# An attention and soft-MoE kernel: q and first-layer weights in longer packets, 32x32 score tiles, single ranks, late turning of combine weights

## The chip, the cores and the metric

One core of one Trainium2 chip. The metric is the device time in microseconds of one launch, the median of the runs shown. The engines are named as in the profile: PE (TensorE matmuls; PEld its weight loads), DVE (VectorE), ACT (ScalarE), POOL (GpSimd), SP (SyncE, which issues all DMA transfers here).

## The reference

```python
# q, k, v: [8 batches, 8 heads, 576, 64]; phi: [8, 8, 576, 32]; float32
a = softmax(phi, axis=2)                      # over the 576 tokens
k_m, v_m = a^T k, a^T v                       # 32 memory slots per head
attn = softmax(q k_m^T / 8, axis=-1)          # over the 32 slots
x = heads side by side of attn v_m            # [4608 tokens, 512]
logits = x @ moe_phi                          # [4608, 32]: 8 experts, 4 slots each
slot_input = softmax(logits, axis=0)^T x      # over all tokens
slot_out[e] = relu(slot_input[e] @ w1[e]) @ w2[e]    # w1: 512 x 1024, w2: 1024 x 512
out = softmax(logits, axis=1) @ slot_out      # [4608, 512]
```

## The kernel before

Every step is handed to a planner (`Plan.add`) with an engine, a cost, the tiles that it reads and writes and a rank. The planner walks through a modelled time and writes out one fixed order of instructions for each engine; ready steps of one engine go by rank. Ranks come from the table `AT` and from counters. The engines then run in that order and wait on semaphores. All DMA transfers stand on SP's queue, in the planner's order, and a load waits there until its buffer is free.

*Attention.* The 8 batches are worked in 4 pairs. A batch has phi, k, v and q loaded (`load_phi`, `load_kv`, `load_q`), 128 partitions by 4 chunks c of two heads each; 64 partitions hold one head, 9 tokens (j) each. phi's maximum is taken on DVE, spread by PE and ACT, subtracted on POOL and exponentiated on ACT (`shifted`); POOL adds up the sums (`summed`). `pooled` (L704) makes the 32 memory keys and values of each head on 64x32 PE tiles and ACT scales them into kp and vm. `turned` transposes kp (L748) and vm (L755), ACT copies them out (L762, L771), and PE multiplies the values by the routing matrix (L781). q is turned in blocks of 32x32 by DVE (`turn_q`, L591). For each pair and each chunk c, `scores` (L813) gives 128 partitions by 2 x 288 scores: 8 matmuls on 64x64 tiles, where the keys stand twice in a block-diagonal form (kps, whose other blocks are set to zero at the start), because the 64 partitions of one head hold two halves of its tokens. `softmax` takes it through DVE, POOL, ACT and back, `logits` (L882) sums the routing logits, and `route` weighs the tokens of a pair into the slot inputs (L1010, L1046, L1054, L1085). After the last pair, DVE merges the four pairs into SIM (L1233), the slot inputs of all experts.

*Experts.* 16 first-layer tiles of 1 MB (`expert_in`, L1353), 11 second-layer tiles of 1 MB (`expert_out`, L1413) and 5 more in quarters of 256 KB (`tail_out`, `tail_mult`), first the left 256 columns of the output (d = 0, in kvbank), then the right ones (d = 1, in scbank). The tiles share the arena, into which the weights are loaded as the attention's buffers come free. With each of the last six whole second-layer tiles a filler matmul (`keep_warm`, L1399) is handed in at a late rank.

*Output.* `slots` makes the combine weights of a pair, has PE turn them (L1523: five transposes a pair) and has ACT cast them into cT (L1535, L1538, L1539). `slot_sums` sums one half of the columns (L1325); then PE multiplies by the combine weights (L1594), ACT and DVE copy the results out (L1570, L1571) and SP stores them (L1607, L1687): six groups of three rows of tokens left, the same six right, then 18 rows whole.

Of the kernel before, what the change touches and what calls it, by code (L numbers as in the profile page):

```python
# [17 lines left out]
FILL = 10 ** 6  # L18
# [252 lines left out]
def kernel(  # L271
# [72 lines left out]
    KP_W = R * (P + Y)  # L344
# [65 lines left out]
    kbs, vTs = stack([2, C, R, M], 4, fifo=True), stack([C, R, M], 2)  # L410
# [33 lines left out]
    NWARM = 40  # L444
# [53 lines left out]
    DMA_RATE, IN_RATE, HALF_RATE, SPREAD = 412e3, 386e3, 350e3, 1.0  # L498

    def load(dst, src, nbytes, w, pri=None):  # L500
        add(
            SP, 0.06, lambda: nc.sync.dma_start(dst(), src), w=[w],  # L502
            dma=nbytes / {1 << 20: DMA_RATE, 1 << 18: HALF_RATE}.get(nbytes, IN_RATE), pri=pri, slack=SPREAD if nbytes == 1 << 18 else 0.0,
        )


    FIRST = ["phi0.0", "phi1.0", "mphi", "q0.0", "k0.0", "v0.0", "q1.0", "k1.0", "v1.0"]
# [30 lines left out]
    add(POOL, 3.6, f, r=[mphi_b], w=[mphd_b])  # L538
# [6 lines left out]
    class Batch:  # L545
# [32 lines left out]
        def load_q(self, u):  # L578
            qt, c0, c1 = self.qt, u * self.ks, u * self.ks + self.ks
            load(  # L580
                lambda: qt.ap.rearrange("p (c x) -> p c x", c=C)[:, c0:c1],
                rows(q, self.b)[:, c0:c1], H * S * D * 4 / self.units,
                qt if self.units == 1 else qt.part(u), pri=first(f"q{self.b}.{u}"),
            )
# [107 lines left out]
        def pooled(self, u):  # L692
# [6 lines left out]
            def f(js):  # L699
                for j in js:  # L700
                    for c in range(c0, c1):
                        for a in range(2):
                            h0 = HALF * a
                            nc.tensor.matmul(  # L704
                                acc.ap[M * c: M * c + M, a, : 2 * D],
                                ph()[h0: h0 + HALF, c, j, :],
                                kv()[h0: h0 + HALF, :, c, j * D: j * D + D],
# [5 lines left out]
            for js in (range(0, 3), range(3, 6), range(6, 9)):  # L713
                add(
                    PE, (0.075 * len(js) * self.ks, 8 * len(js) * self.ks), lambda f=f, js=js: f(js),
                    r=[pt.part(u), kvt.part(u), kvt.part(self.units + u)], w=[acc], also=[kp, vm],
                )

            def f():
                for a in range(2):  # L720
                    nc.scalar.activation(
                        kp.ap[o: o + n].rearrange("p i (r x) -> p i r x", r=R)[:, :, :, HALF * a: HALF * a + Y],
                        acc.ap[o: o + n, a, :D].rearrange("p (i x) -> p i x", i=2).unsqueeze(2)
                        .to_broadcast([n, 2, R, Y]),
                        AF.Copy, scale=rs.ap[o: o + n, a: a + 1],
                    )
                for a in range(2):
                    nc.scalar.activation(  # L728
                        vm.ap[o: o + n, a], acc.ap[o: o + n, a, D: 2 * D], AF.Copy,
                        scale=rs.ap[o: o + n, a: a + 1],  # L730
                    )

            add(
                ACT, 2 * act(P) + 2 * act(D), f, r=[acc, rs.part(u)],
                w=[kp.part(u), vm.part(u)],
            )

        def turned(self, u, vpb):
            kp, vm, kd, vT, n, o, g = self.kp, self.vm, self.kd, self.vT, self.n, u * self.n, self.g
            c0, c1, ks = u * self.ks, u * self.ks + self.ks, self.ks  # L740
            tp, tv, vpp = b_m.tile(), b_m.tile(), b_m.tile()
            ii = ident[o: o + n, o: o + n]

            def f():
                x = tp.ap.rearrange("p (i c r m) -> p i c r m", i=2, c=C, r=R)
                for i in range(2):
                    for r in range(R):
                        nc.tensor.transpose(  # L748
# [389 lines left out]
    for bp in range(NBP):  # L1138
# [19 lines left out]
        for h in range(2):  # L1158
            plan.at(bp + at["turn"][h])
            for x in pair:  # L1160
                x.turn_q(h)
# [530 lines left out]
```

## Time and profile before

| | |
|---|---|
| median of 3 runs | 202.4 us (202.2 to 202.49) |
| the profiled execution: time, span | 202.39 us, 200.6 us |
| PE, DVE, POOL, ACT busy | 172.5, 134.4, 84.3, 70.3 us |
| moved by DMA | 76.47 MB, mean 381 GB/s |
| mean granted clock of TensorE | 0.973 |

A row of a view gives start, duration, engine, line and operation, output tile and input tile; in brackets how long the engine stood idle before it and what ended that. A tile's name is that of its buffer: nearly all SBUF tiles lie in `arena`. A matmul in float32 runs in two passes, so it stands as two records of PE and two of PEld; transposes stand as one. DMA share is the mean busy share of the core's 16 DMA engines; where packets overlap it goes over 1.

### The profile page before, as it was taken

To read this page: it belongs to the slowest core of one execution; us is meant where nothing else is said; L and a number is where in the kernel's file an instruction comes from. 1 tells how busy PE (TensorE), PEld (TensorE's weight loads), DVE (VectorE), ACT (ScalarE), POOL (GpSimd) and SP (SyncE) were. 2 spreads that over 40 slices of the span, in tenths; PEclk is the share of its full clock that TensorE was granted. 3 is DMA by queue.
4 is the path that set the end of the run, shared out by engine and by line. 5 is a ranking of instruction groups with operands and counts; after the bars stand their busy time and mean duration, and the time that the engine had idled before them with its cause. 6 is when DMAs were issued, how large, how long until landed. Compare 5 with 4: busy or idle time off the path is not lost.

```text
span 200.6 us, 6083 instructions
## 1 busy us (share of the span) xinstructions
PE 172.5 (86%) x2623; PEld 111.0 (55%) x2623; DVE 134.4 (67%) x243; ACT 70.3 (35%) x188; POOL 84.3 (42%) x84
## 2 busy tenths in 40 slices
PE   7999748978699899797999789799999999999930
PEld 6777534636457387464665347464655654557520
DVE  6822640799897899999899996478990110558810
ACT  2022314546341755607463252110201123356600
POOL 7199204589992994889964276000000000000000
PEclk9999997899969999999999999999999999999995
DMA  5999999999999999999999999999999999999996
GB/s 201 362 394 395 381 384 389 381 390 379 397 379 390 389 382 396 383 391 398 404 412 401 409 408 411 408 430 418 415 418 421 378 321 329 356 331 312 398 426 279
DMA packets 34090, 76.47 MB, mean 381 GB/s; under 512 B 2064, under 2 KB 15888, under 8 KB 32400
## 3 DMA queue, kind: packets, MB, share of 16 engines
q1 hardware_dynamic: 34064, 76.09, 100.7%
q8 instruction: 20, 0.33, 0.7%
q14 instruction: 6, 0.05, 0.1%
HBM read 66.65 MB, written 9.44 MB: 379 GB/s over the span
## 4 chain that ended last, share of the span: by engine, by line
PE 34%; DMA 26%; DVE 13%; POOL 11%; issue 4%; SPq 4%; ACT 2%; POOLq 1%; DVEq 0%
DMA arena<-in_moe_w_dram 18%; DMA arena<-in_v_dram 8%; PE bank L1594 6%; PE scbank L813 6%; PE kvbank L704 5%; SPq L502 4%; PE bank L882 4%; POOL arena L848 3%; POOL arena L669 3%; POOL arena L648 3%; POOL arena L871 3%; PE bank L1010 2%; DVE arena L606 2%; DVE arena L827 2%; DVE arena L874 2%
## 5 line engine op out<-in xcount | busy, mean ns | idle before, releaser
L648 POOL TENSOR_TENSOR arena<-arena 128x1152 f32<-128x1152 f32 x8 | 21.0, 2633 | 17.6 <-ACT arena L641 15.1
L591 DVE STREAM_TRANSPOSE arena<-top 128x1152 f32<-128x1152 f32 x16 | 21.6, 1355 | 8.4 <-DMA top<-in_q_dram 8.4
L704 PE MATMUL kvbank<-arena 64*32 64x128 f32 x1152 | 21.2, 279 | 6.1 <-issue 2.9
L520 PE MATMUL kvbank<-ones 128*128 128x256 f32 x82 | 23.7, 426 | 2.4 <-ACT arena L728 1.3
L813 PE MATMUL scbank<-arena 64*64 64x288 f32 x256 | 23.8, 445 | 2.2 <-DVE arena L827 2.1
L669 POOL TENSOR_TENSOR arena<-arena 128x128 f32<-128x128 f32 (+2 forms) x32 | 23.4, 732 | 3.2 <-ACT arena L657 1.3
L704 PEld LDWEIGHTS kvbank<-arena 64*32 64x32 f32 x1152 | 16.5, 107 | 10.8 <-issue 5.9
L871 POOL TENSOR_TENSOR arena<-arena,ssm 128x576 f32<-128x576 f32 x16 | 18.3, 1155 | 9.5 <-DVE ssm L867 7.9
L848 POOL TENSOR_TENSOR arena<-arena,smx 128x576 f32<-128x576 f32 x16 | 18.4, 1153 | 7.6 <-DVE smx L843 7.6
L882 PE MATMUL bank<-arena 128*128 128x288 f32 x64 | 18.8, 425 | 1.3 <-DVE arena L874 0.8
L606 DVE TENSOR_REDUCE arena<-arena 128x128 f32<-128x1152 f32 x8 | 17.1, 2148 | 3.7 <-DMA arena<-in_phi_dram 3.6
L520 PEld LDWEIGHTS kvbank<-ones 128*128 128x128 f32 x82 | 15.9, 209 | 6.1 <-ACT arena L728 1.7
L1571 DVE COPY arena<-bank 128x256 f32<-128x256 f32 (+1 forms) x30 | 14.2, 510 | 5.9 <-PE bank L1594 5.8
L827 DVE STREAM_TRANSPOSE arena<-scbank 128x576 f32<-128x576 f32 x16 | 12.2, 765 | 5.4 <-PE scbank L813 5.4
L1594 PE MATMUL bank<-sr,cT 64*128 64x256 f32 (+1 forms) x104 | 14.7, 355 | 0.7 <-DVE arena L1571 0.6
L813 PEld LDWEIGHTS scbank<-arena 64*64 64x64 f32 x256 | 9.8, 139 | 10.1 <-DVE arena L827 3.6
L853 ACT ACTIVATE arena<-arena 128x576 f32<-128x576 f32 x16 | 11.0, 685 | 11.2 <-POOL arena L848 11.0
L882 PEld LDWEIGHTS bank<-arena 128*128 128x128 f32 x64 | 11.2, 189 | 6.4 <-issue 1.7
L1353 PE MATMUL bank<-arena,SIM 128*32 128x256 f32 x224 | 13.2, 390 | 0.4 <-DVE SIM L1233 0.4
L1594 PEld LDWEIGHTS bank<-sr,cT 64*128 64x128 f32 x104 | 9.9, 185 | 6.4 <-DVE arena L1571 4.6
L1570 ACT COPY arena<-bank 128x256 f32<-128x256 f32 (+1 forms) x24 | 10.3, 445 | 8.4 <-PE bank L1594 7.0
L874 DVE STREAM_TRANSPOSE arena<-arena 128x576 f32<-128x576 f32 x16 | 11.9, 754 | 1.5 <-POOL arena L871 1.5
(139 smaller groups left out, 249.2 us busy)
## 6 DMA issues: line engine op xcount, KB each, us to landing
arena<-in_moe_w_dram SPq DMA_DIRECT2D x25, 1024.0 KB, 14.5
top<-in_q_dram SPq DMA_DIRECT2D x8, 1152.0 KB, 12.6
arena<-in_k_dram SPq DMA_DIRECT2D x8, 1152.0 KB, 10.1
arena<-in_v_dram SPq DMA_DIRECT2D x8, 1152.0 KB, 12.5
arena<-in_moe_w_dram SPq DMA_DIRECT2D x20, 256.0 KB, 6.0
arena<-in_phi_dram SPq DMA_DIRECT2D x8, 576.0 KB, 7.2
out_dram<-arena SPq DMA_DIRECT2D x11, 384.0 KB, 3.4
out_dram<-arena SPq DMA_DIRECT2D x1, 2304.0 KB, 8.1
```

What stands on the lines that cost most here:

```text
L520: lambda: nc.tensor.matmul(warm.ap, ones, ones.unsqueeze(1).to_broadcast([P, 2, P]), start=True, stop=True,),
L591: lambda: nc.vector.transpose(qT.ap.rearrange("p (i u y) -> p u i y", i=2, y=Y), qt.ap[:, h * QT_SZ: h * QT_SZ + QT_SZ].rearrange("p (u i ...
L606: lambda: nc.vector.tensor_reduce(mx.ap[:, c0:c1], ph().rearrange("p c j m -> p c m j"), axis=AX.X, op=ALU.max),
L648: lambda: nc.gpsimd.tensor_tensor(ph(), ph(), mb.ap[:, c0:c1].unsqueeze(2).to_broadcast([P, c1 - c0, J, M]), op=ALU.subtract,),
L669: plus = lambda o, x, y: nc.gpsimd.tensor_tensor(o, x, y, op=ALU.add)
L704: nc.tensor.matmul(acc.ap[M * c: M * c + M, a, : 2 * D], ph()[h0: h0 + HALF, c, j, :], kv()[h0: h0 + HALF, :, c, j * D: j * D + D], start= ...
L813: nc.tensor.matmul(scb.ap[HALF * g: HALF * g + HALF, a, :JY], pair[g].kd.ap[h0: h0 + HALF, i, c].rearrange("p r m -> p (r m)"), pair[g].qT ...
L827: lambda: nc.vector.transpose(ex.ap[:, c * PART: (c + 1) * PART].rearrange("p (a x) -> p a x", a=2), scb.ap[:, :, :JY],),
L848: lambda: nc.gpsimd.tensor_tensor(exv(), exv(), bc(mx), op=ALU.subtract),
L871: lambda: nc.gpsimd.tensor_tensor(exv(), exv(), bc(sm), op=ALU.mult),
L882: nc.tensor.matmul(lp.ap[:, :JY], vpb.ap[:, h, :], aT.ap[:, a * JY: (a + 1) * JY], start=(h == 0), stop=(h == H - 1),)
L1594: nc.tensor.matmul(po.ap[:, : x.stop - x.start], cT[bp].ap[y: y + HALF, j // 2 * P: j // 2 * P + P], sr.ap[y: y + HALF, t, x], start=(t == 0),
```

## The change

q is read so that 32 partitions hold one head, 18 tokens each in one run of 4608 bytes, four heads to each of two halves of the tile. The scores of a chunk then take 16 matmuls on 32x32 tiles, the keys are needed once and not in a block-diagonal form, and the order of the tokens changes within a column of the scores (`by_row`, `by_token` put it right where the combine weights are copied out). First-layer weights are read two rows to a partition, 8192 bytes, and the last product of `route` writes the slot inputs in the order that fits. `turned` is split into keys and values. Each pair has its own row of ranks in `AT`, with more entries; the first loads stand in another order; `keep_warm` is gone; the combine weights of pairs 2 and 3 are turned after a group of the output and not ahead of it, through one bank. The planner's costs for the changed steps and its DMA rates are adapted, and NWARM is 47 for 40.

```diff
-    KP_W = R * (P + Y)
+    KP_W = P
...
-    kbs, vTs = stack([2, C, R, M], 4, fifo=True), stack([C, R, M], 2)
+    kbs, vTs = stack([2, C, M], 4, fifo=True), stack([C, R, M], 2)
...
-        for a in kps.aps:
-            nc.vector.memset(a, 0.0)
...
-    FIRST = ["phi0.0", "phi1.0", "mphi", "q0.0", "k0.0", "v0.0", "q1.0", "k1.0", "v1.0"]
+    FIRST = [
+        "v1.0",
+        "phi0.0",
+        "v0.0",
+        "phi1.0",
+        "k0.0",
+        "q0.0",
+        "mphi",
+        "q1.0",
+        "k1.0",
+    ]
...
         def load_q(self, u):
+            src = q[self.b].rearrange("h (p j) y -> (h p) (j y)", j=U)
             load(
-                lambda: qt.ap.rearrange("p (c x) -> p c x", c=C)[:, c0:c1],
-                rows(q, self.b)[:, c0:c1], H * S * D * 4 / self.units,
+                lambda: qt.ap.rearrange("p (t x) -> p t x", t=2),
+                src.rearrange("(t r) x -> r t x", r=P), H * S * D * 4,
...
     def scores(c, pair, ex):
...
             for i in range(2):
-                for a in range(2):
-                    for g in range(2):
-                        h0 = HALF * a
-                        nc.tensor.matmul(
-                            scb.ap[HALF * g: HALF * g + HALF, a, :JY],
-                            pair[g].kd.ap[h0: h0 + HALF, i, c].rearrange("p r m -> p (r m)"),
...
-                            tile_position=(h0, HALF * g),
+                for r in range(R):
+                    for a in range(2):
+                        for g in range(2):
+                            k, x = HALF * (c % 2) + Y * a, HALF * g + M * r
+                            nc.tensor.matmul(
+                                scb.ap[x: x + M, a, :JY],
+                                pair[g].kd.ap[k: k + Y, i, c],
...
+                                tile_position=(k, x),
...
         sip = b_m.tile()
...
-            for a in range(2):
+            for z in range(2):
                 for g in range(2):
-                    nc.tensor.matmul(
-                        sip.ap[HALF * a: HALF * a + HALF, :P],
-                        pair[g].vm.ap[:, a, :],
-                        wtb.ap[:, g, a].rearrange("p c n -> p (c n)"),
+                    for u in range(2):
+                        for a in range(2):
+                            x = HALF * u + NS * a
+                            nc.tensor.matmul(
+                                to[x: x + NS, z],
+                                pair[g].vm.ap[:, a, z::2],
+                                wtb.ap[:, g, a, u::2],
...
-            turn=(0.504, -0.618),
-            chunk=(0.032, 0.327, 0.478, 0.492),
+            turn=(48.615, 26.283, 20.725, 43.051),
+            chunk=(0.648, 12.747, 13.934, 26.056),
+            soft=(9.192, 13.22, 1.61, 1.477),
...
-        at = AT[(bp > 0) + (bp == NBP - 1)]
+        at = AT[bp]
...
-    TURN = {1: 0, 2: 0, 3: 1}
+    TURN, LATE = {1: 0}, {2: 5, 3: 7}
...
-        w1v = w1[e].rearrange("(c p) f -> p c f", p=P)
-        w1b = [load_w(w1v[:, 2 * i: 2 * i + 2], wqs if e == EG else ws) for i in range(2)]
+        w1v = w1[e].rearrange("(i p z) f -> i p (z f)", i=2, z=2)
+        w1b = [load_w(w1v[i], wqs if e == EG else ws) for i in range(2)]
...
-            if 2 * e + i >= 2 * E - NT - 6:
-                keep_warm([t])
...
+    def turn(bp, after):
+        csb = turned[bp]
...
-            tp = b_m.tile()
+            tp = cool if bp in LATE else b_m.tile()
...
     for n in range(-1, NA):
         if n >= 0:
             z = half_group(0, n, n == 0)
+            for bp in LATE:
+                if LATE[bp] == n:
+                    turn(bp, [z])
...
     for n in range(NA):
-        half_group(1, n)
+        z = half_group(1, n)
+        for bp in LATE:
+            if LATE[bp] == NA + n:
+                turn(bp, [z])
```

More of the change, by code (lines that the diff above doesn't have):

```diff
@@ L443 @@
     )
-    NWARM = 40
+    NWARM = 47
     NTAIL = 3
@@ L714, in pooled @@
                 add(
-                    PE, (0.075 * len(js) * self.ks, 8 * len(js) * self.ks), lambda f=f, js=js: f(js),
-                    r=[pt.part(u), kvt.part(u), kvt.part(self.units + u)], w=[acc], also=[kp, vm],
+                    PE, ((0.075 if y1 - y0 == 2 else 0.05) * len(js) * self.ks, 8 * len(js) * self.ks),
+                    lambda f=f, js=js: f(js),
+                    r=[pt.part(u), *(kvt.part(y * self.units + u) for y in range(y0, y1))],
+                    w=[acc], also=[kp, vm][y0:y1],
@@ new lines, in turned_k, with turned_v @@
+            add(PE, (0.27, 4), f, r=[kp.part(u), ident_b], w=[tp], also=[kd])
+            add(
+                ACT, act(2 * n),
+                lambda: nc.scalar.copy(
+                    kd.ap[:, :, c0:c1].rearrange("p i c m -> p i (c m)"),
+                    tp.ap[:, : 2 * C * M].rearrange("p (i c m) -> p i c m", i=2, c=C)[:, :, c0:c1]
+                    .rearrange("p i c m -> p i (c m)"),
+                ),
+                r=[tp], w=[kd.part(u)],
+            )
+        def turned_v(self, u, vpb):
+            vm, vT, n, o, g = self.vm, self.vT, self.n, u * self.n, self.g
+            c0, c1, ks = u * self.ks, u * self.ks + self.ks, self.ks
+            tv, vpp = b_m.tile(), b_m.tile()
+            ii = ident[o: o + n, o: o + n]
@@ L1122 @@
-            chunk=(0.106, 0.219, 0.401, 0.611),
-            logit=(-2.612, -2.214, -1.572, -0.776),
-            route=1.408,
+            phi=(-19.641, -3.117),
+            max=(-1.978, 3.292),
+            kv=(18.924, -1.896),
+            sum=(-7.49, -13.974),
+            pool=(-1.888, -2.303),
+            vals=(-0.668, 22.259),
+            q=(6.85, 12.507),
+            turn=(32.072, 26.603, -3.564, 37.829),
+            chunk=(-0.283, 7.098, 5.25, 7.311),
+            soft=(-7.457, 13.114, 14.519, 8.353),
@@ new lines @@
+            sum=(9.252, 8.262),
+            pool=(4.273, 21.368),
+            vals=(-30.988, -5.667),
+            q=(16.403, -3.726),
+            turn=(14.098, 26.025, 13.999, 12.368),
+            chunk=(-7.491, -5.414, -6.142, -25.901),
+            soft=(-0.668, -20.009, 6.975, 6.254),
+            logit=(0.067, 10.182, 3.487, -4.149),
+            route=1.926,
+        ),
+        dict(
+            phi=(-6.622, -13.368),
+            max=(-9.325, 3.33),
+            kv=(1.63, -8.403),
+            sum=(5.489, 3.599),
+            pool=(5.965, -2.814),
+            vals=(11.124, 21.77),
+            q=(10.204, -18.837),
+            turn=(7.536, 18.578, 16.523, 31.437),
+            chunk=(2.239, -17.343, -4.856, 6.534),
+            soft=(3.112, 4.03, 1.985, 0.428),
+            logit=(12.857, -10.598, 18.142, 7.604),
+            route=5.226,
@@ L1503, in slots @@
             add(
-                ACT, act(ND * P), lambda: nc.scalar.copy(c4.ap, t4.ap[:, : ND * P]),
+                ACT, act(ND * P),
+                lambda: nc.scalar.copy(by_token(c4.ap), by_row(t4.ap[:, : ND * P])),
                 r=[t4], w=[c4],
```

182 lines of the change are left out of this document (90 added, 92 removed).

## The prediction, made before the changed kernel ran

> **What bounds the kernel now.** First the page's DMA rows, then the busy time by stretches, then the chain that ended last, then the timeline of TensorE at the two places where the chain is on it.
>
> ```profile
> DMA  5999999999999999999999999999999999999996
> DMA packets 34090, 76.47 MB, mean 381 GB/s; under 512 B 2064, under 2 KB 15888, under 8 KB 32400
> q8 instruction: 20, 0.33, 0.7%
> ```
>
> The DMA engines are at nine tenths or more in every slice but the first and the last. The next rows (columns: stretch, its length, busy time of PE, PEld, DVE, ACT, POOL with their instruction counts, granted clock, DMA share, GB/s) give the rates.
>
> ```profile
> 8.00:90.00 82.00, 69.60 (x1428) 47.35 (x1426) 58.92 (x86) 33.73 (x86) 56.53 (x52) 0.96 1.06 388
> 98.00:128.00 30.00, 26.85 (x341) 16.98 (x333) 26.18 (x44) 11.00 (x36) 15.62 (x15) 1.00 1.03 408
> 132.00:155.00 23.00, 22.33 (x339) 13.31 (x338) 16.57 (x44) 3.05 (x9) 0.00 (x0) 1.00 1.01 419
> 160.00:172.00 12.00, 11.89 (x141) 6.28 (x135) 2.19 (x5) 3.14 (x11) 0.00 (x0) 1.00 1.01 329
> 176.00:178.00 2.00, 2.00 (x17) 1.38 (x16) 0.93 (x3) 1.61 (x5) 0.00 (x0) 1.00 0.93 315
> 180.00:182.00 2.00, 1.78 (x17) 1.33 (x16) 1.48 (x6) 1.04 (x3) 0.00 (x0) 1.00 0.75 252
> 182.00:188.00 6.00, 5.78 (x37) 4.10 (x36) 5.05 (x11) 3.68 (x9) 0.00 (x0) 1.00 1.02 346
> ```
>
> With the share at 1 or above throughout, the rate still follows the run of bytes that one packet takes: 388 GB/s while the inputs flow (1152 and 2304 bytes a packet, by the source patterns), 408 with first-layer weights (4096), 419 with second-layer weights (8192), 329 with the quarter tiles (1024). Only two stretches fall clearly below: 0.93 and 0.75, worth about (0.09 + 0.27) x 2 = 0.7 us against the 1.02 of the next row. So transfer time is what the kernel mostly pays; the chain says where computing touches it.
>
> ```profile
> 162.34 5.93 DMA arena<-in_moe_w_dram
> 168.32 0.63 PE kvbank L1413 x6
> 168.95 0.63 PE scbank L1399 x2
> 169.58 0.61 PE bank L1325 x2
> PEld kvbank L1413 <- DMA arena<-in_moe_w_dram: 1.1, 2, 0.6
> 136.72 7.58 PE L1353 MATMUL bank<-arena,SIM 128*32 128x256 f32 x128 [0.40 <-DVE SIM L1233]
> ```
>
> TensorE starts the expert layers at 136.72, when the slot inputs (SIM) are ready, and works without a gap until the last left-half weights land at 168.28; over the whole run it waits for weights only 1.1 us. Both run almost level: the end follows whichever is later, the bytes or SIM.
>
> **The change part by part.** *Packets.* q goes from 2304 to 4608 bytes, first-layer weights from 4096 to 8192.
>
> ```profile
> top<-in_q_dram SPq DMA_DIRECT2D x8, 1152.0 KB, 12.6
> arena<-in_moe_w_dram SPq DMA_DIRECT2D x25, 1024.0 KB, 14.5
> top<-in_moe_w_dram SPq DMA_DIRECT2D x2, 1024.0 KB, 10.9
> ```
>
> q is 8 x 1152 KB = 9.44 MB. Of the 27 whole weight tiles 16 are first-layer: 16.78 MB. First layer: 16.78/408 - 16.78/419 = 41.1 - 40.0 = 1.1 us. q: no row has 4608 bytes; the nearest is 4096 at 408, so 9.44/388 - 9.44/408 = 24.3 - 23.1 = 1.2 us. Bounds for q: 0, if the 388 is held down by phi's smaller packets alone, and 1.8 at 419. Sum 2.3 us, from 1.1 to 2.9. A loss is excluded: every step up in packet size in these rows is a step up in rate. [...]
>
> The bytes are also reordered. On SP, whose one queue carries all transfers, the first pair's loads stood like this before:
>
> ```order
> L502 DMA arena<-in_phi_dram 128x4x288 x2
> L502 DMA arena<-in_moe_phi_dram 128x4x32
> L502 DMA top<-in_q_dram 128x4x576
> L502 DMA arena<-in_k_dram 128x4x576
> L502 DMA arena<-in_v_dram 128x4x576
> ```
>
> and now
>
> ```order
> L500 DMA arena<-in_phi_dram 128x4x288
> L500 DMA arena<-in_v_dram 128x4x576 x2
> L500 DMA arena<-in_phi_dram 128x4x288
> L500 DMA arena<-in_k_dram 128x4x576
> L500 DMA top<-in_q_dram 128x2x1152
> L500 DMA arena<-in_moe_phi_dram 128x4x32
> ```
>
> One q before the first batch's pooling becomes one v, and the routing matrix comes after it; the pair's last load is k in place of v, behind the same bytes. Pooling of batch 1 starts as before, less the two faster q's (0.3 us).
>
> *Scores.* A chunk is 16 matmuls on 32x32 tiles, eight tiles at a time, for 8 on 64x64, four at a time.
>
> ```profile
> L813 PE MATMUL scbank<-arena 64*64 64x288 f32 x256 | 23.8, 445 | 2.2 <-DVE arena L827 2.1
> L704 PE MATMUL kvbank<-arena 64*32 64x128 f32 x1152 | 21.2, 279 | 6.1 <-issue 2.9 <-ACT arena L657 2.2 <-DMA arena<-in_v_dram 1.0
> L1010 PE MATMUL bank<-arena 64*32 64x288 f32 x144 | 6.9, 411 | 0.7 <-ACT ssm L863 0.4 <-issue 0.3
> L748 PE MATMUL bank<-ident,arena 128*128 128x128 f32 x32 | 5.2, 286 | 1.5 <-ACT arena L721 1.5
> L762 ACT COPY arena<-bank 128x512 f32<-128x512 f32 x8 | 4.6, 581 | 4.3 <-PE bank L748 4.1
> L771 ACT COPY arena<-bank 128x256 f32<-128x256 f32 x8 | 3.0, 375 | 0.0
> ```
>
> Before, a chunk is 256/16 = 16 records (each matmul runs in two passes), 23.8/256 = 93 ns each, 1.49 us. After, it is 32 records. L704, eight tiles of 128 columns, takes 21.2/1152 = 18.4 ns a record, 41 ns for 288 columns, 1.33 us a chunk; L1010, eight tiles and 288 columns, takes 6.9/144 = 48 ns, 1.53 us. So -0.2 to +0.1 us a chunk; I take 0, since each tile streams as many columns as before. The keys' transposes halve: 16 of 32 records at 5.2/32 = 0.16 us, -2.6 us of TensorE over eight batches, and the copy shrinks from 581 to about 375 ns, so a batch's scores are ready some 0.5 us sooner. What grows is the number of instructions, a rival below.
>
> *Slot inputs.* The route's last product becomes 16 matmuls (32 records of 64 columns) for 4 (8 of 128).
>
> ```profile
> L1085 PE MATMUL bank<-arena 128*64 128x128 f32 x32 | 2.7, 285 | 0.3 <-DVE arena L1065 0.3
> L1497 PE MATMUL bank<-ident,L 128*32 128x128 f32 x16 | 0.6, 272 | 0.0
> ```
>
> Before: 2.7/4 = 0.68 us. After: on tiles like L1497's, 0.6/16 = 38 ns at twice the columns, so 0.6 us if columns set it and 1.2 if the count does. I take +0.2 on the path to SIM; three of the four are beside other work. The first q's, the 0.3 us, and the 0.5 us of the batch before SIM cover it. SIM also depends on the new ranks, which reorder VectorE and GpSimd; their work is the same. I take SIM where it was, with 2 us either way as its ordinary bounds.
>
> *Tail.* On TensorE, left half, before (L1413 are the experts' second layer, L1523 the turning of combine weights, L1399 a fill):
>
> ```order
> L1523 MATMUL bank_63<-ident,cS 128x128 x3
> L1413 MATMUL kvbank<-arena 32x256 x4
> L1523 MATMUL bank_62<-ident,cS 128x128
> L1523 MATMUL bank_62<-ident,cS 64x128
> L1413 MATMUL kvbank<-arena 32x256 x4
> L1523 MATMUL bank_64<-ident,cS 128x128 x3
> L1523 MATMUL bank_63<-ident,cS 128x128
> L1523 MATMUL bank_63<-ident,cS 64x128
> L1413 MATMUL kvbank<-arena 32x256 x8
> L1399 MATMUL scbank<-ones 128x256
> L1325 MATMUL bank_65<-cS,rep 128x256
> ```
>
> After, the same stretch, from the turning of pair 1 on:
>
> ```order
> L1584 MATMUL bank_62<-ident,cS 128x128 x3
> L1584 MATMUL bank_63<-ident,cS 128x128
> L1584 MATMUL bank_63<-ident,cS 64x128
> L1463 MATMUL kvbank<-arena 32x256 x16
> L1385 MATMUL bank_65<-cS,rep 128x256
> ```
>
> Two pairs' turning and one fill have left the path to the first slot sums.
>
> ```profile
> 163.73 1.10 PE L1523 MATMUL bank<-ident,cS 128*128 128x128 f32 x8
> 165.33 0.44 PE L1523 MATMUL bank<-ident,cS 128*128 128x128 f32 x2
> 166.26 0.77 PE L1523 MATMUL bank<-ident,cS 128*128 128x128 f32 x5
> 177.69 1.13 PE L1399 MATMUL scbank<-ones 128*128 128x256 f32 x4
> L1535 ACT CAST cT<-bank 128x384 fp32r<-128x384 f32 x4 | 1.9, 481 | 8.9 <-PE bank L1523 8.9
> L1538 ACT CAST cT<-bank 128x128 fp32r<-128x128 f32 x4 | 1.1, 271 | 0.3 <-PE bank L1523 0.3
> L1539 ACT CAST cT<-bank 64x128 fp32r<-64x128 f32 x4 | 1.1, 264 | 0.0
> ```
>
> Ten of the 15 transposes are 2.31 x 2/3 = 1.5 us. With the 1.1 us that TensorE still waits, it can follow weights that land 2.6 us earlier from an unmoved SIM: enough for 2.3. The fill (0.63 us) sat between the last landing and the sums, so stores are ready 0.6 us sooner. The turning comes back among the right-half groups: 1.5 us where a fill of 1.1 us goes, and six casts on ScalarE of 2 x (0.48 + 0.27 + 0.26) = 2.0 us. They now write with a stride, which no row shows: 2.0 if that is free, 4.0 if it doubles. ScalarE is busy 3.68 of 6 us in 182:188, so 2.0 fits and 4.0 nearly does; what hides it is the DMA share of 1.02 there. If the cover fails, the hole at 180:182 stays (0.5 us). I take 0.3 of the 0.7 us of holes as gained. The startup memsets that go cost nothing: VectorE waits for phi anyway.
>
> *Sum*, against the profiled execution's 202.39 us (span 200.6 and 1.8 around it; the median of the runs is 202.4, so nothing is to be shifted): 202.4 - 2.3 - 0.3 = 199.8 us.
>
> **The rivals.** *TensorE is short of instructions; slower.* It rests on these rows:
>
> ```profile
> PE 172.5 (86%) x2623; PEld 111.0 (55%) x2623; DVE 134.4 (67%) x243; ACT 70.3 (35%) x188; POOL 84.3 (42%) x84
> 30.57 0.66 PE L704 MATMUL kvbank<-arena 64*32 64x128 f32 x28 [2.88 <-issue]
> 33.00:112.00 79.00, 71.15 (x1377) 45.79 (x1375) 70.24 (x107) 38.92 (x104) 60.88 (x55) 0.96 1.05 392
> 70.00:80.00 10.00, 10.00 (x210) 7.76 (x209) 9.60 (x16) 5.57 (x20) 7.17 (x9) 1.00 1.05 387
> ```
>
> In the midst of batch 1's pooling, 144 matmuls in a row, TensorE stood 2.88 us with nothing to wait for. Queue 8 brings 20 packets, 0.33 MB, for 2 x 2623 instructions: about 260 each, through the same full DMA engines. 33:112 carries 1377 + 1375 = 2752 matmuls and weight loads, 35 per us; 70:80, where TensorE never stops, 42. The change adds 14 chunks x 32, two slot products x 48 and takes away 8 batches x 4: +512, so 41 per us, all but the best rate seen. Two more stalls like that row on the way to SIM, 5.8 us, less the 0.3 and 0.5 us that the batches gain, put SIM 5 us late; the tail takes up 0.3 (2.6 - 2.3): 199.8 + 5 - 0.3 = 204.5. From a SIM more than 3.3 us late the run is slower than before. For it: the stall. Against: TensorE is idle for 7.9 of the 79 us, and the halved transposes free 2.6 more. [...] Chance 0.20.
>
> *The scoring stage gives back part.* A little of the same, or an order of VectorE (70.24 of 79 us busy) with more gaps, puts SIM 1.3 to 2.5 us late: 200.9 to 202.0. Chance 0.16.
>
> *Packets are worth nothing.* If the rates of the three stretches come from what else runs then, not from packets, only the holes go: 202.1, no change. Against it: share 1.01 to 1.06 in all. Chance 0.08.
>
> *SIM earlier.* If the ranks also bring SIM 2 us forward, all holes close and q reaches its 1.8: 198.8. Chance 0.04.
>
> **How the numbers follow.** Forecast 199.8, chance 0.52, own range 199.2 to 200.9. What a measurement can tell from no change is 0.2%, 0.4 us. Faster: 0.52 + 0.16 + 0.04 = 0.72; same 0.08; slower 0.20. The range goes from 199.0 to 204.2: below lies most of the 0.04, above about 0.10.
>
> **What would show it.** Right: q's and first-layer stretches at about 405 to 410 and 419 GB/s; the last left-half weights landing near 166; SIM at 136 to 137; share near 1 in 174 to 182. Wrong: "issue" waits of TensorE growing past 10 us with SIM after 139; rates unchanged; stores waiting on ScalarE's casts.

## The result and the profile after

| | before | after |
|---|---|---|
| median | 202.44 us (202.2 to 202.51, 4 runs) | 215.69 us (211.49 to 221.01, 4 runs) |
| the profiled execution: time, span | 202.39, 200.6 us | 218.18, 216.4 us |
| mean granted clock | 0.973 | 0.863 |
| first expert matmul (SIM ready) | 136.72 us | 154.79 us |
| from there to the end of the span | 63.9 us | 61.6 us |

The change makes the kernel slower: ratio 1.0491, 95% interval 1.0417 to 1.0565, where the prediction said 199.8 us. The four runs lie far apart, and the time goes with the granted clock: 0.908 with 211.49, 0.879 with 213.21, 0.863 with 218.18, 0.845 with 221.01; the ratio leaves out the two slowest, which may have been disturbed, and by it the loss is 9.9 us. The profile below is of the run with 0.863, so its delays are larger than those behind the 9.9 us; the faster two (0.879 and 0.908, against 0.973 before) lose clock too.

From the page of the changed kernel: the granted clock and the DMA share in 40 slices, the packets, and the queue that brings instructions.

```profile
PEclk9999985667965555999859969999999999999975
DMA  6999999999899899199990998899999999889995
DMA packets 29997, 76.52 MB, mean 354 GB/s; under 512 B 2064, under 2 KB 15888, under 8 KB 26256
q8 instruction: 23, 0.38, 0.7%
```

The packets grew as meant (26256 under 8 KB, 32400 before). But the DMA row now has holes, and the clock row has 5 and 6 where attention is computed. The time up to SIM, by stretches, first before, then after (columns as in the prediction):

```profile
20.00:136.70 116.70, 99.74 (x1740) 64.43 (x1738) 94.48 (x160) 48.74 (x137) 70.46 (x65) 0.97 1.05 395
```

```profile
20.00:154.80 134.80, 116.05 (x2079) 72.24 (x2077) 96.97 (x161) 47.70 (x138) 72.50 (x67) 0.81 0.92 355
62.00:85.20 23.20, 22.66 (x321) 12.77 (x320) 15.57 (x24) 8.46 (x21) 15.62 (x16) 0.50 0.97 364
115.00:120.00 5.00, 4.21 (x161) 3.31 (x159) 4.97 (x9) 1.62 (x5) 4.77 (x6) 1.00 0.18 33
155.00:170.00 15.00, 15.00 (x258) 9.29 (x254) 12.23 (x31) 2.05 (x5) 0.00 (x0) 1.00 1.01 419
```

In both traces the granted clock is either 1.00 or 0.50, so a mean of 0.81 over 134.8 us is 51 us at half clock, against 7 us before (twice what is missing to 1.00). In one stretch, 62 to 85.2, TensorE works almost without a pause (22.66 of 23.2 us) and has half the clock all the while. VectorE and GpSimd have the work of before (96.97 for 94.48 us, 72.50 for 70.46). DMA stands nearly still in 115:120 (0.18): there SP's queue stands 14.0 us behind one wait for PE. From SIM to the end it takes no longer than before (61.6 for 63.9 us).

What TensorE waits for, and two chunks of scores in the timeline:

```profile
PE scbank L831 <- issue: 4.4, 2, 2.5
PE kvbank L713 <- issue: 3.9, 2, 2.0
```

```profile
44.85 2.16 PE L831 MATMUL scbank<-arena 32*32 32x288 f32 x29 [1.97 <-issue]
...
59.91 1.42 PE L831 MATMUL scbank<-arena 32*32 32x288 f32 x32
...
77.12 2.17 PE L831 MATMUL scbank<-arena 32*32 32x288 f32 x32
```

"issue" is time in which nothing that the profile shows was waited for: 8.3 us in four waits, 3.2 in two before. The first row is one of them, with the half clock behind it. A chunk takes 1.42 us at full clock, about what was forecast, and 2.17 at half. SIM is 18 us late. TensorE's busy time from 20 us to SIM is 16.3 us longer (116.05 for 99.74), its idle time only 1.8 us (18.75 for 16.96): the issue waits grew by 5.1 us, but other waits shrank. So nearly all of the delay is work that takes longer, with 51 us at half clock for 7.

### The profile page after: what moved, and what is told of

It reads as the page before. It is cut to its first block, busy times and chain, and to the rows that moved or that the text cites. A ratio compares the mean times of both kernels' runs of the same rounds, so it can differ in the third digit from the quotient of the medians.

```text
span 216.4 us, 6726 instructions
## 1 busy us (share of the span) xinstructions
PE 184.4 (85%) x2949; PEld 117.1 (54%) x2949; DVE 136.2 (63%) x241; ACT 68.8 (32%) x188; POOL 84.8 (39%) x84
## 2 busy tenths in 40 slices
DMA packets 29997, 76.52 MB, mean 354 GB/s; under 512 B 2064, under 2 KB 15888, under 8 KB 26256
## 4 chain that ended last, share of the span: by engine, by line
PE 64%; DMA 7%; DVE 7%; issue 6%; SPq 4%; POOL 3%; ACT 3%; POOLq 1%; ACTq 0%; DVEq 0%
PE scbank L831 11%; PE bank L900 9%; PE kvbank L713 8%; DMA arena<-in_k_dram 7%; PE bank L1413 7%; PE bank L1657 6%; SPq L500 4%; PE kvbank L1463 3%; PE scbank L1463 3%; PE bank L1028 2%; PE bank L798 2%; PE bank L639 1%; POOL arena L678 1%; PE kvbank L528 1%; POOL arena L657 1%
## 5 line engine op out<-in xcount | busy, mean ns | idle before, releaser
L831 PE MATMUL scbank<-arena 32*32 32x288 f32 x512 | 28.4, 530 | 4.4 <-issue 4.4
L713 PE MATMUL kvbank<-arena 64*32 64x128 f32 x1152 | 24.2, 307 | 5.4 <-issue 3.9
L528 PE MATMUL kvbank<-ones 128*128 128x256 f32 x84 | 24.9, 436 | 2.2 <-ACT arena L741 1.1
L900 PE MATMUL bank<-arena 128*128 128x288 f32 x64 | 25.2, 540 | 0.3 <-DVE arena L892 0.2
L713 PEld LDWEIGHTS kvbank<-arena 64*32 64x32 f32 x1152 | 18.9, 117 | 10.7 <-issue 6.8
L528 PEld LDWEIGHTS kvbank<-ones 128*128 128x128 f32 x84 | 16.9, 216 | 6.2 <-ACT arena L741 1.5
L900 PEld LDWEIGHTS bank<-arena 128*128 128x128 f32 x64 | 15.1, 254 | 7.9 <-issue 2.8
L831 PEld LDWEIGHTS scbank<-arena 32*32 32x32 f32 x512 | 10.1, 125 | 14.6 <-issue 11.5
L871 ACT ACTIVATE arena<-arena 128x576 f32<-128x576 f32 x16 | 10.9, 683 | 9.4 <-POOL arena L866 9.4
L666 ACT ACTIVATE arena<-arena 128x1152 f32<-128x1152 f32 x8 | 9.3, 1165 | 9.3 <-POOL arena L657 9.2
L861 DVE TENSOR_REDUCE smx<-arena 128x18 f32<-128x576 f32 x16 | 11.9, 746 | 0.3
## 6 DMA issues: line engine op xcount, KB each, us to landing
arena<-in_k_dram SPq DMA_DIRECT2D x8, 1152.0 KB, 10.2
```

The costliest lines, as they stand in the source:

```text
L528: lambda: nc.tensor.matmul(warm.ap, ones, ones.unsqueeze(1).to_broadcast([P, 2, P]), start=True, stop=True,),
L713: nc.tensor.matmul(acc.ap[M * c: M * c + M, a, y0 * D: y1 * D], ph()[h0: h0 + HALF, c, j, :], kv()[h0: h0 + HALF, y0:y1, c, j * D: j * D + D],
L831: nc.tensor.matmul(scb.ap[x: x + M, a, :JY], pair[g].kd.ap[k: k + Y, i, c], pair[g].qT[c // 2].ap.rearrange("p (i r x) -> p i r x", i=2, r=R)[
L900: nc.tensor.matmul(lp.ap[:, :JY], vpb.ap[:, h, :], aT.ap[:, a * JY: (a + 1) * JY], start=(h == 0), stop=(h == H - 1),)
```

## The experiments

Four theories were put to the test. *Tile*: tiles of 32x32, eight at a time, work on half of the array (8 x 32 x 32 of the 128*128 that the largest tiles of the profile cover), and the granted clock answers to that. *Supply*, the rival on record: TensorE runs out of instructions. *Place*, which came up after the first runs: what counts is where the blocks of 256 instructions end, which the kernel's planner counts (`BLOCK`). *Order*: the new ranks make a worse order. In the table "issue" is the sum of PE's issue rows in the waits view, and the clock is the mean from 20 us to SIM, both of the profiled execution.

| run | median us | ratio to before (95%) | SIM at | issue us | clock |
|---|---|---|---|---|---|
| before | 202.4 to 202.9 | | 136.7 | 3.2 | 0.97 |
| after | 215.69 | 1.049 (1.042 to 1.057) | 154.8 | 8.3 | 0.81 |
| wide_tiles | 207.56 | 1.025 (1.019 to 1.030) | 145.1 | 12.6 | 0.89 |
| old_ranks | 217.77 | 1.074 (1.068 to 1.081) | 153.6 | 5.5 | 0.86 |
| split_scores | 213.70 | 1.055 (1.054 to 1.057) | 149.0 | 10.9 | 0.92 |
| w1_packets | 206.02 | 1.020 (1.015 to 1.025) | 141.5 | 5.9 | 0.96 |
| packets_only | 200.93 | 0.991 (0.988 to 0.994) | 136.2 | 2.8 | 0.99 |
| half_rows | 205.67 | 1.018 (1.010 to 1.026) | 141.2 | 3.0 | 0.92 |
| few_wide | 206.56 (202.92 to 209.04) | none given | 139.5 | 3.1 | 0.94 |
| few_wide_sip | 207.65 | 1.022 (1.017 to 1.027) | 145.5 | 6.5 | 0.89 |
| shift64 | 211.67 | 1.046 (1.040 to 1.052) | 144.2 | 10.0 | 0.96 |
| shift128 | 206.88 | 1.019 (1.015 to 1.023) | 140.9 | 5.1 | 0.96 |
| after_shift128 | 210.16 | 1.037 (1.034 to 1.040) | 147.2 | 2.9 | 0.87 |
| late_turns | 203.04 | 1.0022 (1.0010 to 1.0034) | 136.6 | 3.5 | 0.97 |
| few_replanned | 211.29 | 1.041 (1.037 to 1.046) | 148.2 | 5.7 | 0.88 |
| after_wide_shift128 | 207.32 | 1.023 (1.017 to 1.029) | 144.8 | 5.8 | 0.92 |
| w1_planned | 215.57 | 1.067 (1.061 to 1.072) | 150.4 | 7.0 | 0.91 |
| w1_same_pe | 205.44 | 1.013 (1.010 to 1.015) | 140.6 | 4.9 | 0.96 |
| w1_same_pe_pool | 205.73 | 1.013 (1.010 to 1.017) | 141.4 | 5.0 | 0.96 |
| w1_view | 201.68 | 0.997 (0.995 to 0.999) | 136.5 | 3.3 | 0.99 |

From SIM to the end of the span all of them take 60.8 to 64.6 us, at most 0.7 more than before (63.9): the losses of over 2 us are made before SIM.

### The tile

wide_tiles: the changed kernel with 64x64 tiles, as many instructions in the same order.

```diff
-                            k, x = HALF * (c % 2) + Y * a, HALF * g + M * r
+                            k, x, w = HALF * a, HALF * g, JY // 2
...
-                                scb.ap[x: x + M, a, :JY],
-                                pair[g].kd.ap[k: k + Y, i, c],
+                                scb.ap[x: x + HALF, a, w * r: w * r + w],
+                                pair[g].kd.ap[k: k + HALF, i, c // 2 * 2: c // 2 * 2 + 2].rearrange("p c m -> p (c m)"),
...
-                                    k: k + Y, i, r, :
+                                    k: k + HALF, i, c % 2, w * r: w * r + w
```

> The changed kernel, all instructions in the same order and number, but each of the 16 score matmuls of a chunk is a full 64x64 tile of 144 columns instead of a 32x32 tile of 288, so that all of TensorE's rows and columns work (the scores come out of the wrong columns; nothing else differs). Three theories. Tile: the granted clock falls because eight 32x32 tiles fill half the array; then the clock keeps to about the 0.96 of before and the time goes to 199 to 204 us. Supply (the rival on record): PE runs out of instructions, 64 a chunk as here; then it stays at 211 to 221 us with PE's issue waits as long as in the changed kernel. Order: the single ranks put work where PE must wait; then it also stays at 211 to 221 us.

5.0 us less than after by the two ratios (8 by the medians), but not 199 to 204: the tile makes half of the loss in this order, and the issue waits are even longer (12.6 us). half_rows puts the same question to the kernel before, whose order and number of instructions stay:

```diff
-                            pair[g].kd.ap[h0: h0 + HALF, i, c].rearrange("p r m -> p (r m)"),
+                            pair[g].kd.ap[h0: h0 + Y, i, c].rearrange("p r m -> p (r m)"),
...
-                                h0: h0 + HALF, i, c % 2, :
+                                h0: h0 + Y, i, c % 2, :
```

> The kernel before in its own order with as many instructions, each score matmul on a tile of 32 rows by 64 columns instead of 64x64 (it leaves out half of each sum), so that 8 of the array's 16 blocks of 32x32 work, as in the changed kernel. Tile theory, by the array's share alone: the granted clock falls to 0.90 or less and the time goes to 206 to 216 us. Supply: nothing is added, 202 to 203 us with the clock as before (0.96). If the clock falls only where PE has just starved, this run too stays at 202 to 203.

half_rows, the stretch to SIM, and the group of the scores:

```profile
20.00:141.20 121.20, 105.56 (x1743) 67.89 (x1743) 94.38 (x160) 48.51 (x137) 70.43 (x65) 0.92 1.04 392
```

```profile
L813 PE MATMUL scbank<-arena 32*64 32x288 f32 x256 | 24.6, 464 | 2.0 <-DVE arena L827 2.0
```

Nothing was added and the issue waits are those of before (3.0 us), yet the clock over the stretch falls from 0.97 to 0.92, some 20 us at half clock for 7, and SIM comes 4.5 us later; the records of the scores take 464 ns for 445. The clock fell less than tile said (0.92, not 0.90 or less) and the time stays below its 206 to 216: the effect is there, and smaller than expected.

Where the clock falls says more. Each of the stretches at half clock on the way to SIM, first of before, then of half_rows, begins after a pause of TensorE:

```profile
32.70:36.20 3.50, 3.50 (x23) 1.64 (x22) 0.22 (x1) 1.63 (x4) 2.62 (x1) 0.51 1.07 379
56.60:60.10 3.50, 3.50 (x66) 2.00 (x59) 3.38 (x6) 1.16 (x2) 3.42 (x4) 0.51 1.06 379
```

```profile
32.00:42.40 10.40, 10.40 (x169) 6.80 (x177) 4.33 (x5) 3.97 (x9) 6.75 (x7) 0.51 1.06 386
59.30:62.80 3.50, 3.50 (x63) 2.47 (x58) 3.50 (x4) 1.00 (x3) 3.36 (x4) 0.51 1.05 397
117.40:124.30 6.90, 6.90 (x59) 3.39 (x51) 5.32 (x11) 2.11 (x6) 4.61 (x5) 0.51 1.03 410
```

The first follows the same issue wait in both (2.9 and 2.6 us), and lasts 3.4 us with full tiles and 10 with half-filled ones. The second follows a pause of 1.46 us in both. The third, in half_rows alone, follows a pause that before has too and comes out of at full clock:

```profile
114.92 1.20 PE L813 MATMUL scbank<-arena 64*64 64x288 f32 x16 [1.06 <-DVE arena L827]
```

```profile
117.01 1.87 PE L813 MATMUL scbank<-arena 32*64 32x288 f32 x16 [1.06 <-DVE arena L827]
```

The changed kernel's long stretch, 61.6 to 85.6 us, compares in the same way with wide_tiles, which has its order and full tiles and is back at full clock by 64:

```profile
60.40:64.00 3.60, 3.60 (x47) 2.95 (x49) 1.76 (x3) 2.49 (x4) 3.60 (x4) 0.53 1.05 394
64.00:85.60 21.60, 19.09 (x483) 13.53 (x483) 20.30 (x34) 10.72 (x31) 18.97 (x19) 1.00 1.01 380
```

In after_shift128, a run with 32x32 tiles that comes up below, the clock is lost even without a pause: TensorE works on from 111.9 us, and at 119.0 goes from full to half.

```profile
115.70:119.00 3.30, 3.30 (x68) 2.46 (x76) 1.85 (x3) 0.82 (x5) 0.22 (x1) 1.00 1.01 427
119.00:122.50 3.50, 3.50 (x30) 1.92 (x10) 3.47 (x5) 0.68 (x1) 1.24 (x2) 0.51 1.02 424
```

So in these runs a pause cost the clock with full tiles too (wide_tiles has 27 us at half clock before SIM); with half-filled tiles it stayed down longer (10 us for 3.4 behind the same wait), and was lost where full tiles kept it (at 117.4 us in half_rows).

### The number of instructions

split_scores: before, with each score matmul cut into two of half the columns.

```diff
+            for r in range(R):
...
-                            scb.ap[HALF * g: HALF * g + HALF, a, :JY],
+                                scb.ap[HALF * g: HALF * g + HALF, a, w * r: w * r + w],
```

> The kernel before in its own order, each 64x64 score matmul cut into two of 144 columns: 64 PE instructions a chunk as in the changed kernel, the same columns and the same full array. Supply: issue waits of PE grow as in the changed kernel (some 10 us in sum) and the time goes to 206 to 216 us. Tile and order: 202 to 204 us, the clock as before.

```profile
PE kvbank L704 <- issue: 6.8, 5, 2.4
PE scbank L814 <- issue: 4.1, 3, 2.9
```

Supply is borne out: 10.9 us of issue waits and 11.2 us more time, with the full array. The clock falls here too (0.92): it goes to half at 31.1 and 44.7 us, at two of the waits, which end at 30.8 and 44.8, and later behind other pauses. So clock was lost behind waits for instructions too, but little of it in shift64 below, which has 10.0 us of such waits and a clock of 0.96. Yet in the order of the changed kernel the number counts for little. few_wide has half the score instructions of wide_tiles, few_wide_sip also the old 4 matmuls of the slot-input product; the cut shows few_wide against after:

```diff
-                for r in range(R):
...
-                                scb.ap[x: x + M, a, :JY],
+                                scb.ap[x: x + HALF, a, :JY],
...
-                                pair[g].kd.ap[k: k + Y, i, c],
+                                pair[g].kd.ap[k: k + HALF, i, c // 2 * 2: c // 2 * 2 + 2].rearrange("p c m -> p (c m)"),
...
-                                    k: k + Y, i, r, :
+                                    k: k + HALF, i, c % 2, :
```

> The changed kernel in its own order, with 8 score matmuls a chunk on 64x64 tiles of 288 columns as the kernel before has (the scores come out of the wrong columns): against the run with 16 of 144 columns (wide_tiles, 207.6 us) only the number of instructions differs, 64 a chunk against 32. Supply: the issue waits of PE fall from 12.6 us to 3 to 6 and the time to 199 to 203 us. If the number of instructions is not what the other run waited for, it stays at 206 to 208.

> The run few_wide with the slot-input product in the 4 matmuls a pair of the kernel before too (its rows then don't fit the weights' order): the changed kernel without any PE instruction that the change adds. Supply: as little issue wait as before (3 us), and so the time that the prediction's other terms give, 199.8 us (199.0 to 201). The 48 matmuls of the slot-input product cost what it is below few_wide: 0.5 to 3 us by the w1_packets run, 0.2 by the prediction.

few_wide_sip has none of the instructions that the change adds to the scores and to the slot-input product (2597 matmul records for 2623 before), and takes 207.65 us, as long as wide_tiles. Its waits:

```profile
PE kvbank L713 <- issue: 5.4, 2, 3.7
PE bank L639 <- DVE pmh L630: 3.4, 1, 3.4
PE bank L623 <- DVE arena L615: 3.1, 4, 1.2
```

A stall of 3.7 us with fewer instructions than before cannot come from their number alone. few_wide lies between 202.92 and 209.04 in four runs and decides nothing.

### Where the blocks end

Queue 8 brings 20 packets before and 23 after, for 2 x 2623 and 2 x 2949 records of PE and PEld: one for 262 and one for 256. The kernel's planner counts blocks of 256, with 6 us from the end of one to the end of the next at the least (`BLOCK`, `BLOCK_US = 6.0`). The shift runs add 64 or 128 instructions at the start, by cutting fills in two, and leave the order alone.

```diff
-                lambda: nc.tensor.matmul(
-                    warm.ap, ones, ones.unsqueeze(1).to_broadcast([P, 2, P]),
...
+            for x in ((0, P), (P, 2 * P)) if j < 16 else ((0, 2 * P),):    # j < 32 for 128
+                nc.tensor.matmul(
+                    warm.ap[:, x[0]: x[1]], ones,
...
```

> The kernel before in its own order, with 16 of the fill matmuls of the start (before 25 us) cut into two of 128 columns: 64 more PE instructions in a place where PE only fills, so that every later instruction stands 64 further in its block of 256. Place theory: PE starves where two block ends come close together in a run of short matmuls, so the time moves with the place alone, by 1 to 5 us either way, and the issue waits come at other lines. Count theory: what counts is only how many instructions the scoring stage has; 202.4 to 203 us.

> The same with 32 fill matmuls cut in two, half a block of 256. Place theory: 1 to 5 us either way from 202.5, and not the time of the shift by 64. Count theory: 202.4 to 203 us.

> The changed kernel in its own order with 32 of its fill matmuls of the start cut in two. Place theory: the changed kernel's 211 to 221 us hang on where the blocks of 256 end, so this run differs from it by over 2 us, either way. Count and tile theories: 211 to 221 us again.

shift64 in the timeline:

```profile
13.68 1.89 PE L519 MATMUL kvbank<-ones 128*128 128x256 f32 x8
15.99 2.16 PE L708 MATMUL kvbank<-arena 64*32 64x128 f32 x134 [0.42 <-DMA arena<-in_v_dram]
22.22 0.43 PE L708 MATMUL kvbank<-arena 64*32 64x128 f32 x10 [4.07 <-issue]
44.86 1.20 PE L817 MATMUL scbank<-arena 64*64 64x288 f32 x14 [3.20 <-issue]
```

64 harmless instructions make the kernel before 9.2 us slower, more than either theory expected; 128 make it 4.4 slower, and the changed kernel 2.5 faster (by the ratios 1.037 and 1.049). The stalls moved to new lines: the first pooling, 144 matmuls in a row, now holds a block end near its end (18.2 us) as well as one at its start. Counted in the trace of before, with ends 64 instructions earlier and the planner's 6 us from one to the next, the estimate is stalls of 4.2 us at 17.9 and 4.0 at 41.3 (40.1 in that trace, and 1.2 later because the first stall is longer); for five of the six issue waits of before and after, the traces have 5.6 to 6.8 us from the block end ahead to the end of the wait, and 9.3 for the sixth. The run has 4.07 at 18.2 and 3.20 up to 44.86.

The traces of all runs say the same. Count the records of PE and PEld in the order in which they start: in before, the two issue waits end after 705 and 3265 records, in shift64 the five end after 449, 1218, 2242, 2498 and 3265. Each of these numbers is 193 or 194 above a multiple of 256, and so are 70 of the 72 issue waits of the twenty runs (the other two are of 0.39 us). The planner's first block of TensorE has 193 instructions (`FIRST_BLOCK`). And all six issue waits of before and after end 1.2 to 1.4 us after a packet of queue 8 has landed (in before one lands at 29.21 and the wait ends at 30.57). So in these runs an issue wait stands at the end of a block, and number and place are two sides of one thing: TensorE waits where it gets through a block sooner than the next one is there. Both shifts make the order of before slower, which fits an order that was planned for its own block ends.

after_wide_shift128 joins the two, and misses its 202: 207.3, 2.8 us below after_shift128 (210.2), and no better than wide_tiles alone. Tile and place don't add up: with this shift the tile is worth 2.8 us, without it 5.0.

> The changed kernel in its order with 32 fills of the start cut in two (after_shift128, 210.2 us) and the 16 score matmuls of a chunk on full 64x64 tiles of 144 columns. If tile and place add up: 8 us below after_shift128 (or 5.5 below wide_tiles' 207.6), 202 us (200 to 204), the clock over 0.93. If the tile costs only where PE starves at the places of the changed kernel: 207 to 210.

### The order

old_ranks puts before's `AT` and `FIRST` into the changed kernel; few_replanned gives few_wide_sip the planner's old costs for the two steps, so that the new ranks are planned for the block ends that are there.

```diff
...
-        at = AT[bp]
+        at = AT[(bp > 0) + (bp == NBP - 1)]
...
```

```diff
-        add(PE, (1.1, 64), f, ...)      # scores
+        add(PE, (1.05, 32), f, ...)
-        add(PE, (0.65, 64), f, r=[wtb, ...)
+        add(PE, (0.5, 16), f, r=[wtb, ...)
```

> The changed kernel (32x32 score tiles, q in 4608-byte packets, 8192-byte weight packets, last pairs turned late) with the load order and the ranks of before. Tile and supply: the clock still falls in the scoring stage, 208 to 221 us. Order: the time comes back to 199 to 204 us.

> The run few_wide_sip (the changed kernel with full-array score tiles and no added PE instruction, its scores and weight rows out of place), with the planner's costs set to the instructions that are really there, so that the order is made anew with the change's ranks for its own block ends. If the 7 us are an order planned for other block ends: 199 to 203 us, issue waits of 3 to 5 us. If they are the ranks: 205 to 209 us, with waits of PE for DVE and ACT as in few_wide_sip.

old_ranks does not help (217.8): with the same tiles, the old ranks are no better than the new. few_replanned is nearly 4 us slower than the run that it was to mend. Neither expectation has it: the issue waits are near the first one's (5.7 us), the time above both.

### The packets and the tail

packets_only and w1_view change the views of the loads and nothing else; w1_packets adds the slot-input product in 16 matmuls that these rows need, w1_planned tells the planner of it, and w1_same_pe gets the rows in place without one more instruction of TensorE (the value columns written evens first, the last addition into SIM in eight parts; three of them on POOL in w1_same_pe_pool).

```diff
-        w1v = w1[e].rearrange("(c p) f -> p c f", p=P)
+        w1v = w1[e].rearrange("(i p z) f -> i p (z f)", i=2, z=2)
...
-        add(PE, (0.5, 16), f, r=[wtb, ...)      # w1_planned only
+        add(PE, (0.65, 64), f, r=[wtb, ...)
...
-        nc.vector.tensor_add(                                      # w1_same_pe only
...
+            (nc.vector if n < 8 else nc.gpsimd).tensor_tensor(     # for eight parts n; n < 5 in w1_same_pe_pool
...
```

> The kernel before in its own order and with its own instructions, with only the two views of the loads changed: q in 4608-byte packets and first-layer weights in 8192-byte packets (the scores and the experts then read rows in the wrong places; no instruction is added). The prediction's sum for the packets alone: 1.2 + 1.1 = 2.3 us less, so 200.1 us (199.6 to 201.3). If the packets are worth nothing here, 202.4; that in the w1_packets run these packets came with 192 more PE instructions, and that those made its 3.5 us, is then shown by the difference of the two.

> The kernel before with only the view of the first-layer weights' loads changed to 8192-byte packets (the experts then read rows in the wrong places; every engine has the instructions of before). By the prediction's sum 1.1 us less: 201.4 us (200.8 to 202.0), the stall near 28 us as before (2.9 us). Then w1_same_pe's loss came from what was added beside the packets. If the packets themselves bring it, 205 to 206 with the stall at 4.2 us.

> The kernel before in its own order with the first-layer weights in 8192-byte packets alone (and the slot-input product in 16 small tiles a pair that these need). By the prediction's sum 1.1 us less for the weights, 0.1 more for the product at the end: 201.4 us (200.9 to 202.4). All three theories expect this; if it is slower by over 1 us, the packets or the small tiles are part of the cause.

> The kernel before with the first-layer weights in 8192-byte packets and the slot-input product in 16 small tiles a pair, the planner told that product's 64 instructions (w1_packets kept the order of before and took 206.0 us). If its 3.5 us were block ends out of their planned places: 201.2 to 203 us, issue waits of PE about 3 us. If the small tiles themselves cost it: 205 to 207 us again.

> The kernel before with the first-layer weights in 8192-byte packets, and PE's instructions and their order unchanged: ACT writes the value columns even rows first, the routing projection is loaded in the same order, and DVE's last addition into SIM is eight additions of 32 partitions that put the rows in place (1.0 us by estimate from the 0.29 us of the one, against it 0.3). The packets' 1.1 us less, the additions 0.5 to 0.8 more: 201.8 to 202.3 us. If the 3.5 us of w1_packets came from the packets and not from PE's instructions, 205 to 206.

> The same with three of the eight additions on POOL: 0.2 to 0.4 us less than w1_same_pe if POOL does them beside DVE, 201.5 to 202.0 us.

packets_only by stretches:

```profile
8.00:90.00 82.00, 68.75 (x1429) 47.10 (x1427) 59.90 (x86) 33.65 (x86) 57.50 (x52) 0.98 1.05 393
98.00:128.00 30.00, 26.41 (x334) 16.77 (x326) 25.94 (x44) 10.98 (x35) 15.13 (x14) 1.00 1.00 413
```

The packets bring 2.0 us by the medians (1.1 to 2.5 by the ratio), 0.8 of it by the weights (w1_view) and so about 1.2 by q; as the difference of two runs that is uncertain by some 0.8. w1_packets loses all of that and more with 192 instructions added. In w1_planned the planner's new order is 9.5 us slower than w1_packets by the ratios, where 3 to 5 us less was expected. w1_same_pe loses twice: its eight additions take longer than estimated, and the stall near 28 us is longer, 4.2 us for 2.9, though TensorE's order is the same:

```profile
32.37 1.09 PE L709 MATMUL kvbank<-arena 64*32 64x128 f32 x28 [4.20 <-issue]
139.67 1.84 DVE L1242 TENSOR_TENSOR SIM<-arena 32x64 f32<-32x64 f32 x8
```

w1_view, with the same packets, does not have the longer loss, so it comes from what stands beside them (the routing projection in four loads, strided copies on ACT); which of them was not tried. POOL's help brought nothing.

late_turns is the end of the change alone: `TURN, LATE = {1: 0}, {2: 5, 3: 7}`, and no `keep_warm`.

> The kernel before with only the end of the change: the last two pairs' combine weights turned between the output multiplications, and no late fills. All before the expert weights' end is as before. The prediction's sum gave this 0.3 us (0.0 to 0.7): 202.2 us. From the runs so far, where the stretch from the first expert matmul to the end fell from 62.7 us (old end) to 61.6 (new end), 1.1 us: 201.4 us.

It loses 0.5 us. First before, then late_turns, columns as above:

```profile
178.00:184.00 6.00, 5.49 (x45) 4.39 (x44) 4.35 (x12) 2.96 (x9) 0.00 (x0) 1.00 0.93 313
```

```profile
178.00:184.00 6.00, 5.51 (x42) 3.67 (x41) 3.50 (x10) 4.19 (x14) 0.00 (x0) 1.00 0.85 284
```

The last left-half weights land at 168.4 us as before (168.28), and the slot sums begin no sooner (169.62 for 169.49). The turning that comes back among the output groups leaves a deeper hole there (0.85 for 0.93; ScalarE busy 4.19 of 6 us for 2.96). Where SIM is late, the stretch behind it takes 62.7 us in split_scores and half_rows, and 61.6 in after. That the same edit gains there, because then TensorE and not the bytes is what the end waits for, is likely but was not tried alone.

No run that computes the whole result beats the kernel before.

## Why the prediction was wrong

- *Packets*: right. 2.3 us forecast, 2.0 measured (1.1 to 2.5), about 1.2 of it by q as forecast (with an uncertainty of 0.8, so that so close a match is partly chance), 0.8 for 1.1 by the first-layer weights. In the changed kernel the bytes are not what the end waits for (DMA share 0.92 on the way to SIM); what the packets are worth there was not measured.
- *Scores*: here it failed. "-0.2 to +0.1 us a chunk; I take 0, since each tile streams as many columns as before" is right at full clock. The prediction read the granted clock in its rows (0.96 to 1.00) and took it for given. At 0.50 a chunk takes 2.17 us. wide_tiles shows what the tile costs in this order, 5.0 us; half_rows shows that the clock answers to the tile with nothing else changed (0.92 for 0.97); and from 64 to 85.6 us (1.00 in wide_tiles, 0.50 in after) the two kernels differ most.
- *"I take SIM where it was, with 2 us either way as its ordinary bounds"*: failed too; SIM came 18 us late in the profiled execution, 16.3 us of it busy time of TensorE. Apart from the tile, few_wide_sip is 6.3 us slower by the ratios than packets_only, from which it differs mainly in the order and the tail, and also in half of the keys' transposes and seven more fills at the start. From before one comes to after by -1.8 (packets, 0.991), 6.3 (order and tail, 1.022), 0.5 (number of instructions in this order, 1.025; not clear of noise) and 5.0 (tile, 1.049): the 9.9 us lost. This is one path; after_wide_shift128 shows that the steps depend on each other.
- *The rival "TensorE is short of instructions"*: it came true in part. "Two more stalls like that row on the way to SIM, 5.8 us": after has two more and 5.1 us. Issue waits "growing past 10 us with SIM after 139" were its mark; SIM came at 154.8 with 8.3 us. But TensorE's idle time to SIM grew by only 1.8 us, so the stalls are not what made SIM 18 us late; what they add through the clock, which fell behind two of them in split_scores (at 31.1 and 44.7 us), was not measured apart from the tile.
- *Its measure*, instructions per us over long stretches, was too coarse: shift64, with the same instructions in the scoring stage, shows that the place of the block ends decides. The issue waits are 10.0 us in shift64, 6.8 more than before, in a run that takes 9.2 us longer.
- *Tail*: -0.3 forecast, +0.5 measured alone (ratio 1.0010 to 1.0034). The step "stores are ready 0.6 us sooner" is what late_turns contradicts: its slot sums begin at 169.62 us, 169.49 before. The stride of the casts, for which the prediction had no row, costs little: 0.50 to 0.53 us in after for 0.48 of the largest.

What stays open: why the order of the changed kernel costs 6.3 us with no instruction added to the scores or the slot inputs. Its issue waits are 3.7 us longer than those of packets_only, and its clock is lower (0.89 for 0.99): 27 us at half clock on the way to SIM for 3.4. The longest issue wait, 3.66 us, ends at 106.4, where the longest stretch at half clock (10.2 us) begins. But few_replanned, planned for its own block ends, is no better, and no run took the waits out of this order.

## What to carry to other kernels

Before an edit that makes matmul tiles smaller or more numerous, price the granted clock too: ask how much of the array the new tiles fill (half-filled ones took it from 0.97 to 0.92 in half_rows), and what TensorE's stage costs at half clock (a chunk of scores 2.17 us for 1.42 in after). Where rows of short matmuls run, the place of each block of 256 instructions is part of the tuning; 64 added instructions far upstream cost 9.2 us in shift64, more than the work they do. Test a part of such a change with the instruction stream held fixed: the new orders that were planned here (w1_planned, few_replanned) moved the time by more than the packets gained.

## What the runs showed of the hardware

- The granted clock stayed at half while TensorE worked almost without a pause: 0.50 from 62 to 85.2 us in after, busy 22.66 of 23.2 us. The two stretches at half clock of before on the way to SIM last 3.4 us each, this one, with 32x32 tiles, 24 us. With full tiles in the same order (wide_tiles) the clock to SIM is 0.89 for 0.81.
- Waits for instructions took up to 4.2 us at one place (w1_same_pe), stood at the ends of blocks of 256 instructions (70 of the 72 waits), and moved with them: 64 instructions more at the start of the kernel before put them at 18.2 us and up to 44.86, and the run takes 9.2 us longer (shift64).
- With longer packets the rate rose above 2 KB too: 388 to 393 GB/s over the input stretch (8:90) with q's packets at 4608 bytes for 2304 (packets_only), 408 to 413 (packets_only) and 418 (w1_view) in 98:128 with those of the first-layer weights at 8192 for 4096.
- DVE took 0.23 us for an addition of 32 partitions by 64 (1.84 us for eight, w1_same_pe).
